# VectorE's block sums, key copies and additions in another order, and raw products placed ahead, in attention followed by two matrix products

## The chip, the cores and the metric

The kernel runs on one core of a Trainium2 chip. The metric is the device time of one execution in microseconds (us). The kernel before took a median of 229.66 us over 5 runs (229.41 to 230.65). A difference of 0.3%, that is 0.69 us, is about what a measurement of this kernel can tell from no change.

The core has five engines, each with its own queue that it works off strictly in order. TensorE (PE) multiplies matrices: it first loads a 128x128 block as weights (PEld), then streams the other operand past it, and its results land in PSUM, a small memory of 8 banks. VectorE (DVE) and ScalarE (ACT) work element by element and empty PSUM into SBUF, the main on-chip memory. GpSimd (POOL) and SyncE (SP) serve here mostly to start DMA transfers. Engines wait for each other through semaphores.

## The reference

```python
# attention, 4 batches x 8 heads x 768 positions x 64; q, k, v are given as float32
scores = (q @ k^T) / 8
mask   = causal for heads 0, 2, 6 ; causal and (first 4 keys or the last 64 keys) for heads 1, 3, 4, 5, 7
a      = exp(scores - max) / (sum + 1e-9), masked scores at -1e9
x      = (a @ v) with heads side by side: 3072 tokens x 512
# two products
h   = x @ w_in          # 512 x 2048
g   = max(0.01*h, h)
out = g @ w_out         # 2048 x 512, float32
```

The kernel computes in bf16 with float32 accumulation.

## The kernel before

**Chunks.** The 3072 tokens are cut into 8 chunks of 384 (half a batch each). `ORDER` (line 57) lists them; "chunk n" is the n-th in that order. Chunks 0 and 1 are the first halves of batches 0 and 1, chunks 2 and 3 their second halves, 4 and 5 the first halves of batches 2 and 3, 6 and 7 their second halves. A chunk goes through three parts.

**Attention of chunk n** (class `Attention`, line 294) is a list of "slots". One slot is a score product (L345 for the heads with full causal attention, L380 for the heads with a window, L325 for the first 4 "sink" keys) into one of two PSUM banks named `psS`, the exponential on ACT (L350, L385, L328), a multiplication with a mask on DVE (L355, L353, L389), and, `lag` slots later, the product with the values (L314) into the banks `po`. When the two heads of one quarter (p = 0 to 3) are done, DVE takes the reciprocal of the sums (L411) and scales (L413, tile `xs`). The result has to be transposed into `xt`: for chunks 1 and 2 by TensorE (L423, emptied by ACT at L425), from chunk 3 on by a DMA on the SP queue (L418).

**Keys and queries.** q, k and v are loaded by POOL's queue (L119, L124) and, from chunk 2 on, turned by DMA transposes on the SP queue (L244): queries into `qd`, keys into `kd`. From `kd` DVE copies the keys into the tiles `kt` that the score products read: six copies of 64x512 per chunk (L253, function `spreads`), and for the first half of a batch two small copies of the sink keys (L278, L282).

**Product 1 of chunk n** (`in_slots`, line 580) is 16 groups of 4 matmuls (L584) into the banks `ph`; ACT applies the leaky ReLU and writes `g_all` (L587). The four matmuls of a group read the four quarters of `xt`, one each.

**Product 2** works on pairs of token tiles of 128. Each chunk has three tiles: two of them make a pair of their own, the third waits for the third tile of the following chunk. So there are 12 pairs: pair 0 from chunk 0, pairs 1 and 2 after chunk 1, pair 3 from chunk 2, pairs 4 and 5 after chunk 3, and so on. Cut into 2x2 blocks, a pair would be eight block products; it is done as seven "units" P1 to P7 in Winograd's way, of 8 matmuls each (L648). They need four sums of the left factor, S1 to S4 (L631, function `sum`, on DVE), and four sums of the weights made once (L609). S2 needs S1, and S4 needs S2. A unit is cut into two steps of 4 matmuls. The units of a pair use three accumulators in PSUM:

- "a": P1, emptied by ACT into `p1` (L667), then P2 on top, emptied by ACT into the output tile `o` (L672);
- "y": P6, emptied by DVE with `p1` added into `u`; then P7 on top, emptied into `u3`; then P4 on top, emptied into `o` (all L663);
- "x": P5, emptied with `u3` added into `o`; then P3 on top, emptied with `u` added into `o`.

So P7 waits until DVE has read P6, P4 until it has read P7, and P3 until it has read P5. P1 and P2 need no sum: they read `g_all` itself ("raw products"). P6 needs S2, P7 S3, P5 S1, P3 S4. Pairs share the two banks `py`. The rows go out by SP's queue (L660).

**What sets the order.** The schedule is written out by hand: every call appends to its engines' queues, in the order of the program. `steps(k, units)` is the list of steps of pair k; `merge(ms, as_)` deals the slots `as_` of the next chunk's attention among the steps `ms` in proportion to costs written at the steps (0.44 for half a unit, 0.65 for a group of product 1); `last_of(ms, us)` gives how many steps are left out at the end, as `keep`, to be run after the attention. A sum of the following pair is emitted after P5, P4 and P3 of a pair (S1, S2, S3), S4 after P1 (line 711 on).

Three stretches matter below:

1. After product 1 of chunk 1: P6, P2, P7, P5, P4, P3 of pair 0 with the key copies of chunk 2 (lines 906 to 910), then S1 to S4 of pair 1 (911), then attention of chunk 2 dealt among 16 steps: pair 1's P6, P7, P5, P4, P3 and pair 2's P1, P6, P2 halves (915 to 918), then the key copies of chunk 3 (919).
2. Attention of chunk 3 beside product 1 of chunk 2, then P5, P4, P3 of pair 2, P1, P6, P2, P7 of pair 3 (`run(outs[:8])`, 940), with the key copies of chunk 4 (`extra`, line 954) emitted ahead of them.
3. Attention of chunk 4 dealt among the groups of product 1 of chunk 3, followed by P5, P4, P3 of pair 3. `last_of(ms, 5.8)` (950) takes P5, P4, P3 and 5 groups out of the dealing.

Of the kernel before, what the change touches and what calls it, by code (L numbers as in the profile page):

```python
# [21 lines left out]
def kernel(  # L22
# [21 lines left out]
    NG = DF // 128  # L44
# [27 lines left out]
    half = one.tile([128, 2], FP32, name="half")  # L72
# [498 lines left out]
    done = [0] * NCH  # L571
# [4 lines left out]
    def costing(us, f):  # L576
        f.us = us
        return f
# [117 lines left out]
    pairs = []  # L696
# [4 lines left out]
        if n % 2:  # L701
            pairs.append(Pair((n - 1, spare(n - 1)), (n, spare(n)), ("psS", "po", "py ph") if end else ("py", "py", "py"), end))

    def steps(k, units=Pair.UNITS, sums=True):

        r = []
        for u in units:
            for half in range(2):
                def step(u=u, half=half):
                    pairs[k].unit(u, half)  # L710
                    if half and u == "P1":
                        if sums:
                            pairs[k].sum(4)
                    if half and 0 < k < len(pairs) - 1 and u in ("P5", "P4", "P3"):
                        pairs[k + 1].sum({"P5": 1, "P4": 2, "P3": 3}[u])
                r.append(costing(0.44, step))
        return r

    def run(*lists):
        for l in lists:  # L720
            for f in l:
                f()
# [175 lines left out]
    for i in range(1, 5):  # L898
        pairs[0].sum(i)
    p1 = in_slots(1, ("ph", "psS"))  # L900
    run(p1[:14], steps(0, ("P1",), False), p1[14:])
    weight_sums(1)
    turn_dma(3)
    load_qk(4)
    load_v(4)
    run(steps(1, ("P1",), False), steps(0, ("P6", "P2", "P7")))
    sp = spreads(2)
    for i, u in enumerate(("P5", "P4", "P3")):
        run(steps(0, (u,)), sp[2 * i : 2 * i + 2])
    run(sp[6:])  # L910
    for i in range(1, 5):
        pairs[1].sum(i)
    run(steps(1, ("P2",)))
    v_shift(3)
    a2, m2 = Attention(2, xt_tag="ph").slots(lag=3), steps(1, ("P6", "P7", "P5", "P4", "P3")) + steps(2)
    m2, outs = m2[:16], m2[16:]
    at = last_of(m2, 2.6)
    run(merge(m2[:at], a2[:-6]), tail(m2[at:], a2[-6:]))
    run(spreads(3))
# [1 line left out]
    for n in range(2, NCH):  # L921
        a, extra = [], ()
        if n + 2 < NCH:
            turn_dma(n + 2)
            v_shift(n + 2)
            extra = spreads(n + 2)
            if ORDER[n + 2][1] == 0:
                load_sinks(ORDER[n + 2][0])
            if n + 3 < NCH:
                load_qk(n + 3, "k" if n > 2 else "kq")  # L930
                if n < 3:
                    load_v(n + 3)
            if ORDER[n + 2][1] == 0:
                sink_values(ORDER[n + 2][0], nc.gpsimd)
        if n + 1 < NCH:
            a = Attention(n + 1, cross=True).slots(lag=2 if n > 2 else 3)
            a = into(a, extra) if n > 2 else a
        ins = in_slots(n)
        if n == 3:
            run(outs[:8])  # L940
            ms = merge(ins, outs[8:8]) + outs[8:]
        else:
            lead = outs[:2] + ins[:2]
            ms = lead + merge(ins[2:], outs[2:-6]) + outs[-6:]
        keep = []
        if n == 2:
            at = last_of(ms, 3.5)
            ms, a, keep = ms[:at], a[:-3], tail(ms[at:-2], a[-3:]) + ms[-2:]
        elif a:
            at = last_of(ms, 5.8)  # L950
            ms, keep = ms[:at], ms[at:]
            if n > 4:
                keep.insert(1, a.pop())
        run(merge(ms, a), keep, extra if n == 2 else ())
        if n in (3, 4):

            nc.gpsimd.tensor_copy(hold[0:1, :], xts[n + 1][0:1, 3, 0:1])
            if n > 2:
                load_qk(n + 3, "q")
            load_v(n + 3)  # L960
        outs = [f for k in range(3 * n // 2, 3 * n // 2 + 1 + n % 2) for f in steps(k)]
# [36 lines left out]
```

## Time and profile before

| | |
|---|---|
| median of 5 runs | 229.66 us (229.41 to 230.65) |
| the profiled execution's own time | 229.72 us |
| its span, first to last instruction | 227.90 us (1.82 us lie around it) |
| granted TensorE clock | 1.00 |
| busy in the span: PE / PEld / DVE / ACT / POOL | 217.2 / 166.4 / 134.6 / 134.6 / 71.4 us |
| a half unit of product 2 (4 matmuls, start to next start) | 0.44 us |
| a group of product 1 (4 matmuls, start to next start) | 0.65 us |
| S1 to S4 on DVE, one | 0.68 us |
| key copy on DVE, median of 36 / longest | 0.29 / 0.93 us |

How to read the lines of the profile: a line of the timeline has start and duration in us, the engine, the line of the kernel, the operation, the tiles written and read, the shape, and how many instructions are merged; in brackets the idle time of the engine ahead of it and whose work ended that. Matmuls overlap, so the time of one is longer than the distance to the next. A DMA's line stands when its queue issues it; when it lands is told as a distance from the issue.

### The profile page before, as it was taken

The numbers are of one execution on the slowest core, as the hardware profiler recorded it, in microseconds if no ns is written. First come the engines' busy times: TensorE is split into PE (matmuls) and PEld (weight loads), VectorE is DVE, ScalarE is ACT, GpSimd is POOL, SyncE is SP. The second block draws the span as 40 slices with busy tenths as digits, with TensorE's granted clock in tenths as the row PEclk, the third lists the DMA queues.
The fourth block names the chain that finished last, engine by engine and source line by source line (L and its number), as shares of the span: only waits on it lengthen the run. The fifth ranks groups of instructions, "written<-read, shape, count | busy, mean of one in ns | idle before, by whom it ended". The sixth has DMA issues, their size and how long they took to land.

```text
span 227.9 us, 5799 instructions
## 1 busy us (share of the span) xinstructions
PE 217.2 (95%) x2344; PEld 166.4 (73%) x2344; DVE 134.6 (59%) x373; ACT 134.6 (59%) x300; POOL 71.4 (31%) x88
## 2 busy tenths in 40 slices
PE   8998899997999999699999999999999999999994
PEld 5687776685788677577688778777777877767893
DVE  7785958948589244948374774454353563600773
ACT  5676856742795996168647543888467774355110
POOL 8978534208508509506080402600000000000000
PEclk9999999999999999999999999999999999999999
DMA  9999999999999999999999991999220032200222
GB/s 130 156 176 168 199 207 174 179 148 135 151 104 271 181 175 152 135 216 160 92 123 153 159 206 25 184 116 151 55 92 3 19 86 60 92 3 0 92 95 92
DMA packets 112970, 29.14 MB, mean 128 GB/s; under 512 B 102960, under 2 KB 110000, under 8 KB 112944
## 3 DMA queue, kind: packets, MB, share of 16 engines
q0 software_dynamic: 77552, 13.37, 86.9%
q1 hardware_dynamic: 34336, 15.14, 35.1%
q8 instruction: 18, 0.29, 0.6%
q10 hardware_dynamic: 1056, 0.26, 0.5%
q14 instruction: 8, 0.07, 0.1%
HBM read 27.30 MB, written 6.29 MB: 147 GB/s over the span
## 4 chain that ended last, share of the span: by engine, by line
PE 80%; DVE 8%; DMA 6%; POOL 2%; issue 1%; ACT 1%; POOLq 0%
PE ph L584 32%; PE py L648 24%; PE po L314 7%; PE psS L345 5%; DMA w_in_bf<-in_moe_w_in_dram 4%; PE po L648 3%; DMA va<-in_v_dram 2%; PE psS L584 2%; DVE sum L631 2%; PE psS L380 2%; DVE kt L253 2%; PE psS L648 2%; PE psS L325 2%; POOL va L124 2%; DVE o L663 1%
## 5 line engine op out<-in xcount | busy, mean ns | idle before, releaser
L584 PE MATMUL ph<-xt,w_in_bf 128*128 128x384 bf16 x448 | 87.8, 326 | 0.4 <-DMA w_in_bf<-in_moe_w_in_dram 0.4
L587 ACT ACTIVATE g_all<-ph 128x384 bf16<-128x384 f32 x112 | 54.9, 490 | 32.6 <-PE ph L584 31.5
L584 PEld LDWEIGHTS <-w_in_bf 128*128 128x128 bf16 x480 | 42.9, 97 | 21.6 <-issue 0.6
L350 ACT ACTIVATE at<-psS 128x384 bf16<-128x384 f32 x78 | 36.8, 490 | 15.3 <-PE psS L345 14.0
L648 PEld LDWEIGHTS <-sum 128*128 128x128 bf16 x400 | 36.8, 98 | 10.6 <-issue 2.6
L119 POOL DMA_DIRECT2D kb<-in_k_dram x21 | 18.8, 914 | 47.3 <-DMA kd<-kb 46.6
L648 PEld LDWEIGHTS <-g_all 128*128 128x128 bf16 x288 | 27.2, 98 | 4.1
L648 PE MATMUL py<-w_out_bf,sum 128*128 128x256 bf16 (+1 forms) x176 | 24.0, 270 | 2.3 <-DVE u L663 2.3
L648 PE MATMUL py<-w_sum,sum 128*128 128x256 bf16 (+1 forms) x176 | 23.9, 270 | 1.2 <-DVE sum L631 1.2
L345 PE MATMUL psS<-qd,kt 128*128 128x384 bf16 (+2 forms) x90 | 22.7, 294 | 0.2
L124 POOL DMA_DIRECT2D va<-in_v_dram x24 | 21.3, 910 | 2.4 <-DMA w_out_bf<-in_moe_w_out_dram 1.8
L663 DVE TENSOR_TENSOR u<-py,p 128x256 f32<-128x256 f32 x20 | 8.4, 421 | 22.2 <-PE py L648 18.8
L119 POOL DMA_DIRECT2D qb<-in_q_dram x21 | 18.7, 910 | 6.1 <-DMA w_in_bf<-in_moe_w_in_dram 2.6
L648 PE MATMUL py<-w_out_bf,g_all 128*128 128x256 bf16 x144 | 20.2, 272 | 0.0
L314 PE MATMUL po<-va,at 128*128 128x65 bf16 x228 | 19.2, 194 | 0.0
L389 DVE TENSOR_TENSOR ats<-ats,m_win 128x384 bf16<-128x384 bf16 x35 | 12.2, 356 | 9.5 <-ACT ats L385 9.1
L385 ACT ACTIVATE ats<-psS 128x384 bf16<-128x384 f32 x35 | 16.6, 488 | 1.8 <-PE psS L380 1.5
L314 PEld LDWEIGHTS <-at 128*128 128x128 bf16 x234 | 14.8, 98 | 3.5
L631 DVE TENSOR_TENSOR sum<-g_all 128x1024 bf16<-128x1024 bf16 x24 | 16.4, 682 | 0.0
L663 DVE TENSOR_TENSOR o<-py,u 128x256 f32<-128x256 f32 (+1 forms) x24 | 9.8, 410 | 10.9 <-PE py L648 10.6
L413 DVE TENSOR_TENSOR xs<-po,linv 128x384 bf16<-128x384 f32 x27 | 15.0, 557 | 0.9
L253 DVE COPY kt<-kd 64x512 bf16<-64x512 bf16 x36 | 12.4, 345 | 2.9 <-DMA kd<-kb 2.5
(168 smaller groups left out, 294.8 us busy)
## 6 DMA issues: line engine op xcount, KB each, us to landing
out_dram<-o SPq DMA_DIRECT2D x23, 256.0 KB, 3.2
va<-in_v_dram POOLq DMA_DIRECT2D x24, 128.0 KB, 8.5
kb<-in_k_dram POOLq DMA_DIRECT2D x21, 128.0 KB, 5.9
qb<-in_q_dram POOLq DMA_DIRECT2D x21, 128.0 KB, 6.5
w_out_bf<-in_moe_w_out_dram POOLq DMA_DIRECT2D x4, 512.0 KB, 12.9
w_in_bf<-in_moe_w_in_dram POOLq DMA_DIRECT2D x3, 512.0 KB, 8.7
vb<-va SPq DMA_DIRECT2D x8, 170.6 KB, 4.2
w_in_bf<-in_moe_w_in_dram POOLq DMA_DIRECT2D x2, 256.0 KB, 7.8
```

The source lines that it names most:

```text
L119: nc.gpsimd.dma_start(out=t[:, g], in_=nat[nm][b, c, :, :, g])
L124: nc.gpsimd.dma_start(out=va[b][:, 3 * c + g, :, 0:D], in_=nat["v"][b, c, :, :, g])
L253: nc.vector.tensor_copy(kt[b % 2][hh][r, :, o : o + 128], raw["kx", n][r, g])
L314: nc.tensor.matmul(o, lhsT=lhsT, rhs=rhs, start=first, stop=False, skip_group_check=True)
L345: nc.tensor.matmul(s[:, off : off + w], lhsT=kt[i][hh][:, p, 128 * kj : 128 * kj + 128], rhs=q_of(n, p, lo, CH), start=(j == 0), stop=(j = ...
L350: nc.scalar.activation(out=a[:, 0:off], in_=s[:, 0:off], func=ACTF.Exp, scale=SM)
L385: nc.scalar.activation(out=av_, in_=s[:, 0:CH].rearrange("p (j e f) -> p j e f", j=3, e=2), func=ACTF.Exp, scale=SM)
L584: nc.tensor.matmul(ph[:, 0:CH], lhsT=w_in_bf[:, g, 128 * t : 128 * t + 128], rhs=xts[n][:, g, :] if n else xts[0][:, :, g, :], start=(g == ...
L587: nc.scalar.activation(out=g_all[:, slab(n) : slab(n) + 3, t, :], in_=ph[:, 0:CH].rearrange("p (j t) -> p j t", j=3), func=ACTF.Prelu, alp ...
L631: nc.vector.tensor_tensor(self.s[i], x, y, op=op)
L648: nc.tensor.matmul(s[:, 0 : c1 - c0], lhsT=lhs[:, j, :], rhs=rhs[:, j, c0:c1], start=first and j == 0, stop=(j == NH - 1), skip_group_chec ...
L663: add = lambda o, t: nc.vector.tensor_tensor(o, s, t[:, c0:c1], op=ALU.add)
```

## The change

The change moves instructions; it adds and removes none. On TensorE 4690 rows of weight loads and matmuls stand in both built programs, on DVE 371, and the rows of the other queues are the same in number; SP and POOL issue the same DMAs in the same order. It has five parts.

- **Sums by a waiting list.** Sums S1 to S3 of the next pair go to a list and are emitted when product 1 of their chunks is complete. S4 of pair k (k > 1) is emitted after P7 of the pair and no longer after P1.
- **Pair 1's S1 and S2** are emitted during pair 0's units, after P2 and P7. S3 and S4 stay where they were.
- **The order of steps beside attention of chunk 2**: pair 2's P1, pair 1's P6, pair 2's P2, pair 1's P7, P5, P4, P3, pair 2's P6. P1 and P2 of pair 2, the raw products, move from places 11 to 12 and 15 to 16 to places 1 to 2 and 5 to 6 of the 16 steps; with them go their two evictions on ACT.
- **Key copies of chunk 4**: four of the six are emitted after pair 3's P2 and so behind DVE's reading of its P6; the other two and the sink copies after P7.
- **P5 of pair 3** is run ahead of product 1 of chunk 3. `ms` is so two steps shorter at its end, and `last_of(ms, 5.8)` now leaves out P4, P3 and 7 groups: attention of chunk 4 is dealt among 9 groups where it was dealt among 11.

```diff
-    def steps(k, units=Pair.UNITS, sums=True):
+    pending = []
+
+    def flush():
+        while pending and all(done[n] == NG for n, _ in pending[0][0].rows):
+            p, i = pending.pop(0)
+            p.sum(i)
+
+    def steps(k, units=Pair.UNITS):
...
                     pairs[k].unit(u, half)
-                    if half and u == "P1":
-                        if sums:
-                            pairs[k].sum(4)
-                    if half and 0 < k < len(pairs) - 1 and u in ("P5", "P4", "P3"):
-                        pairs[k + 1].sum({"P5": 1, "P4": 2, "P3": 3}[u])
+                    if not half:
+                        return
+                    if u == "P7" and k > 1:
+                        pairs[k].sum(4)
+                    if 0 < k < len(pairs) - 1 and u in ("P5", "P4", "P3"):
+                        pending.append((pairs[k + 1], {"P5": 1, "P4": 2, "P3": 3}[u]))
+                    flush()
...
-    run(steps(1, ("P1",), False), steps(0, ("P6", "P2", "P7")))
+    run(steps(1, ("P1",)), steps(0, ("P6", "P2")))
+    pairs[1].sum(1)
+    run(steps(0, ("P7",)))
+    pairs[1].sum(2)
...
-    for i in range(1, 5):
+    for i in range(3, 5):
         pairs[1].sum(i)
...
-    a2, m2 = Attention(2, xt_tag="ph").slots(lag=3), steps(1, ("P6", "P7", "P5", "P4", "P3")) + steps(2)
-    m2, outs = m2[:16], m2[16:]
+    m2 = steps(2, ("P1",)) + steps(1, ("P6",)) + steps(2, ("P2",)) + steps(1, ("P7", "P5", "P4", "P3")) + steps(2, ("P6", "P7", "P5", "P4", "P3"))
+    a2, m2, outs = Attention(2, xt_tag="ph").slots(lag=3), m2[:16], m2[16:]
...
         if n == 3:
-            run(outs[:8])
-            ms = merge(ins, outs[8:8]) + outs[8:]
+            run(outs[:6], extra3[:4], outs[6:8], extra3[4:], outs[8:10])
+            ms = ins + outs[10:]
...
-        run(merge(ms, a), keep, extra if n == 2 else ())
+        run(merge(ms, a), keep)
+        extra3 = extra
```

## The prediction

> **What bounds the kernel now.** I read the page first: TensorE (PE) is busy for 217.2 of 227.9 us, DVE and ACT for 59% each. So only a wait of PE is worth anything. The two longest waits of PE are these:
>
> ```profile
> PE 217.2 (95%) x2344; PEld 166.4 (73%) x2344; DVE 134.6 (59%) x373; ACT 134.6 (59%) x300; POOL 71.4 (31%) x88
> ...
> PE py L648 <- DVE u L663: 2.3, 2, 2.2
> PE py L648 <- DVE sum L631: 1.2, 1, 1.2
> ```
>
> Both lie in the stretches that the change touches. Next the timelines of PE and DVE there. At 55 us PE waits 1.22 us for S1 and S2 of pair 1, which DVE makes behind six key copies; at 95 us it waits 2.16 us because P7 of pair 3 needs DVE's reading of P6 (`u`), which stands behind six key copies and S4:
>
> ```profile
> 54.83 0.69 DVE L631 TENSOR_TENSOR sum<-g_all 128x1024 bf16<-128x1024 bf16 x1
> 55.55 0.69 DVE L631 TENSOR_TENSOR sum<-sum,g_all 128x1024 bf16<-128x1024 bf16 x1
> 56.30 0.61 PE L648 MATMUL py<-w_sum,sum 128*128 128x256 bf16 x4 [1.22 <-DVE sum L631]
> ...
> 93.41 2.44 DVE L253 COPY kt<-kd 64x512 bf16<-64x512 bf16 x6
> 96.63 0.41 DVE L663 TENSOR_TENSOR u<-py,p 128x256 f32<-128x256 f32 x1
> 97.09 1.03 PE L648 MATMUL py<-w_out_bf,sum 128*128 128x256 bf16 x8 [2.16 <-DVE u L663]
> ```
>
> A wait removed is a gain only if nothing later holds PE. So last I looked for what PE meets behind each wait, with the landings of the SP queue's transposes:
>
> ```profile
> L244 SPq DMA_TRANSPOSE qd<-qb x1: 3237/3237/3237, 63.2 to 63.2; - x1
> ...
> DMA to landing us min/median/max: 8.3/8.3/8.3
> ...
> 71.25 0.33 PE L423 MATMUL ph<-ident,xs 128*128 128x128 bf16 x3
> 71.55 0.34 PE L345 MATMUL psS<-qd,kt 128*128 128x384 bf16 x1
> ...
> L418 SPq DMA_TRANSPOSE xt<-xs x4: 1200/1206/2001, 86.6 to 91.3; - x4
> ...
> DMA to landing us min/median/max: 5.5/6.3/7.0
> ...
> 97.97 0.49 PE L345 MATMUL psS<-qd,kt 128*128 128x384 bf16 x3
> 98.29 0.49 PE L584 MATMUL ph<-xt,w_in_bf 128*128 128x384 bf16 x2
> ...
> 108.31 0.36 DVE L389 TENSOR_TENSOR ats<-ats,m_win 128x384 bf16<-128x384 bf16 x1
> ...
> 108.73 0.23 PE L314 MATMUL po<-va,ats 128*128 128x65 bf16 x2
> ...
> 108.99 4.24 PE L584 MATMUL ph<-xt,w_in_bf 128*128 128x384 bf16 x24
> ```
>
> A DMA's line (the views of the tiles `qd` and `xt`) gives the issue, the one below it the time from issue to landing. The queries of chunk 3, issued at 63.25, land 8.3 later at 71.5, and the first score of chunk 3 starts at 71.55, so PE is already held by that DMA (its transposes of `xs` end near 71.42). The last quarter of chunk 3's `xt`, issued at 91.28, lands 7.0 us later (the view narrowed to it), at 98.3; the fourth matmul of the first group, which needs it, starts at 98.29 + 3 x 0.16 = 98.78, half a us later.
>
> **Stretch 1 (55 to 71.5): 0.** S1 and S2 of pair 1 go into DVE's idle times at 49.7 and 51.3 (0.60 and 1.25 us idle in the timeline, against 0.60 us to the next start for a sum), and the first steps beside attention of chunk 2 need no sum. I followed the three queues in the order of the built program with the durations of the rows (score 0.16, half unit 0.44, exponential 0.41 to the next, sum 0.60, 0.2 from PE to a reader, 0.05 back); the same walk over the old order gives the old starts within 0.15 us. PE's wait of 1.22 goes. Part comes back: scores 3 and 4 now wait for the exponentials (0.14 and 0.25); the eviction of P2 on ACT (0.38) holds the bank of a later score (0.18); P6 of pair 2 waits for S2 of its pair, now just ahead of it on DVE (0.25). At the transposes PE is 1.1 us ahead, at about 70.3. There stands the DMA. Its chain (queries of chunk 2 landed at 54.5, POOL's loads from 55.07, landed at 63.1, SP's transpose at 63.25) has no step that PE, DVE or ACT sets, and SP's and POOL's order is unchanged. So the first score of chunk 3 stays at 71.55 and the 1.1 us become a wait at a new place. If the DMA landed sooner, P7 of pair 2 would still wait for `u`, now behind S3 on DVE, until 71.17 instead of 71.72: the bounds are -0.55 and 0, and I take 0, by the row of the landing. S4 of pair 2, now at 73.8 to 74.5, fits ahead of the mask at 74.68.
>
> [...]
>
> **Stretch 2a (94.8 to 98.3): the wait goes, the DMA stays.** `u` is now ahead of the copies: P6 ends at 93.9, `u` runs 94.1 to 94.5, and P7 starts at 94.77, where PE stands, P5 at 95.64, the scores of chunk 4 at 96.51. The second of these needs the fifth copy: four copies (0.31 each) to 95.7, `u3` at 95.84, S4 to 96.8, the copy to 97.1. So PE waits 0.5 there and then for the `xt` quarter: the fourth matmul of the first group starts at 98.30 instead of 98.78, and P5 is already done. If all behind stayed as it is, that were -0.48 - 0.87 = -1.35.
>
> **Stretch 2b (98.3 to 113): it comes back.** Attention of chunk 4 was dealt among groups that covered its chain score, exponential, mask, values. In the built order 10 groups stood ahead of its last value product and 6 behind; now 8 and 8. Where the two are missing PE waits:
> - h2's first score follows the sink product with no group between. Its bank is freed by an exponential of h1, behind the eviction of group 1 on ACT: 0.33; then h1's mask: 0.23. That eats the 0.48.
> - h3's mask stands on DVE behind the reciprocal and scaling of quarter 0 (0.22 + 0.47). It came at 102.82 to 103.18 and the value product at 103.23, with a group at 102.37 as cover. Its score comes no sooner (the same work is ahead of it); the cover of 0.65 is gone: 0.7.
> - h7's mask stands behind four key copies (0.85 and 1.15 a pair) and a scaling. It ended at 108.67, the product started at 108.73 after 0.2 of waiting; with one group fewer ahead: 0.8.
>
> So the last value product of chunk 4 ends at about 109.0, as before. The old 6 groups took 108.99 to 113.06, 0.68 each; two more are +1.36. P5, 0.87, is no longer behind them. Sum: +1.36 - 0.87 = **+0.49**. The same walk over the old order gives P5's start as 113.02 against 113.06, so I trust it to some 0.3 us. Its bounds: no wait added, -1.35; key copies at 0.93, the longest row, +0.8.
>
> The copies: two that ran beside POOL's work took 0.43 to 0.58 each there, against a median of 0.29; without that (0.54 less ahead of the mask of h7), the sum would be -0.05. POOL's work there follows the landing of a DMA and not PE, so I leave them slow.
>
> **The rest: 0.** S4 behind P7 in pairs 4 to 11: P7's reading starts 0.2 after P7, takes 0.34, S4 0.60, P5's reading 0.42, done at 1.57 after P7; P3 starts at 1.74 in the tightest case (P5, P4, P3 without a pause, as at 216). So no wait, 0.17 us to spare. In its old place S4 held no mask that PE waited for. Bounds -0.1 and +0.3.
>
> **Sum.** The profiled execution took 229.72 (span 227.90 and 1.82). +0.49 makes 230.21; it stood 0.06 above the median, so **230.15**, +0.2%. That is inside the 0.3% (0.69 us) that a measurement can tell.
>
> **Rivals.**
> - *Faster: the attention of chunk 4 packs closer than I reckon.* For it: the wait of 2.16 is gone and P5 is filled in. Against it: the walk meets the old times. It decides where the last value product of chunk 4 ends before 107.8; with the -1.35 in full the time is 228.3, with a sum of half the two -0.43, with the landing of stretch 1 besides -0.98: 228.7.
> - *Slower: chunk 3's `xt` lands later.* Its last quarter becomes the gate at 98.3, where there was 0.5 to spare. It is issued by the same steps, but into full DMA queues, and the four of that chunk differ by 1.5 us. Each 0.1 later is 0.1 more: half that spread makes +0.74, 230.9. It decides from a landing at 98.5.
> - *The gain of stretch 1 comes through* because the queries land sooner: 230.15 - 0.55 = 229.6. Against it: nothing in that chain is touched.
>
> **How the numbers follow.** The forecast 0.47 (its own range 229.5 to 230.7), faster rival 0.20, slower rival 0.25, stretch 1 through 0.08. Within 0.3% (228.97 to 230.35): most of the forecast, 0.40, and the last rival, 0.08: 0.48. Slower: 0.25 and 0.07 of the forecast, 0.32. Faster: 0.20. Range 228.7 to 231.0, the faster rival's middle to a little over the slower one's price.
>
> **What would show it.** Right: no PE wait at 55 and at 95; a wait of 1 us or more ahead of chunk 3's first score, which stays near 71.5; P7 of pair 3 right behind P2; a wait at the fourth matmul of product 1 of chunk 3 or the score before it; waits of some 0.7 ahead of value products of chunk 4, eight groups of product 1 in a row behind them, and P4 of pair 3 near 114.4, later than its old 113.94. Wrong: chunk 3's first score before 71, or P4 of pair 3 before 113.3.

## The result, and the profile after

The changed kernel takes 229.71 us (median of 39 executions), the kernel before 230.76 us (65 executions, taken beside them). The ratio is 0.9958, with a 95% interval of 0.9942 to 0.9975: faster by 0.42%, about 0.97 us (0.58 to 1.34). The forecast was 0.49 us slower. The five executions that the forecast started from (median 229.66) lay about a microsecond under the median of the 65, and that turns out to be part of the cause. The ratios leave out executions that took over 1.5% longer than the fastest of the same kernel; in the four sets below these are ten of the kernel before, all at a lower granted clock (0.985 to 0.993), so the ratios rather understate what such a clock costs.

The profile after does not show the gain at first sight. Its span is longer than that of before (227.9). The page, span and busy times:

```profile
span 228.2 us, 5798 instructions
...
PE 217.6 (95%) x2344; PEld 165.5 (73%) x2344; DVE 134.1 (59%) x373; ACT 134.8 (59%) x300; POOL 71.2 (31%) x88
```

The waits of TensorE in the profile after (us in total, times, longest):

```profile
PE po L219 <- DMA kb<-in_k_dram: 1.5, 3, 0.7
...
PE po L314 <- DVE ats L389: 0.8, 2, 0.5
...
PE py L648 <- DVE u L663: 0.6, 1, 0.6
```

The first line lies at 18 to 20 us, in code that the change doesn't touch: the keys of chunk 1 landed later in this execution. So one profile of each kernel can't be compared by the span. I cut each execution at three places on TensorE: the first score of chunk 2, P7 of pair 2, P4 of pair 3. The differences between them are taken from the timelines.

| profile | first score of chunk 2 at | to P7 of pair 2 | to P4 of pair 3 | to the end | mean clock |
|---|---|---|---|---|---|
| before | 54.59 | 17.13 | 42.22 | 113.96 | 1.000 |
| after | 55.63 | 16.56 | 41.90 | 114.11 | 1.000 |

After is 1.04 us late before the change begins, gains 0.57 in stretch 1, gains 0.32 in stretch 2 and loses 0.15 behind. The timeline of TensorE in the profile after, in the two stretches:

```profile
55.63 0.50 PE L345 MATMUL psS<-qd,kt 128*128 128x384 bf16 x2
55.96 0.60 PE L648 MATMUL py<-w_out_bf,g_all 128*128 128x256 bf16 x4
...
71.12 0.33 PE L423 MATMUL ph<-ident,xs 128*128 128x128 bf16 x3
71.28 0.33 PE L345 MATMUL psS<-qd,kt 128*128 128x384 bf16 x1
72.19 0.60 PE L648 MATMUL py<-w_out_bf,sum 128*128 128x256 bf16 x4 [0.58 <-DVE u L663]
...
94.35 1.04 PE L648 MATMUL py<-w_out_bf,g_all 128*128 128x256 bf16 x8
95.23 1.04 PE L648 MATMUL py<-w_out_bf,sum 128*128 128x256 bf16 x8
96.10 1.04 PE L648 MATMUL py<-w_sum,sum 128*128 128x256 bf16 x8
96.97 0.44 PE L345 MATMUL psS<-qd,kt 128*128 128x384 bf16 x2
...
97.64 0.98 PE L584 MATMUL ph<-xt,w_in_bf 128*128 128x384 bf16 x4
...
103.24 0.24 PE L314 MATMUL po<-va,ats 128*128 128x65 bf16 x2 [0.52 <-DVE ats L389]
...
108.37 0.24 PE L314 MATMUL po<-va,ats 128*128 128x65 bf16 x2 [0.30 <-DVE ats L389]
...
108.63 5.63 PE L584 MATMUL ph<-xt,w_in_bf 128*128 128x384 bf16 x32
114.09 1.04 PE L648 MATMUL py<-w_sum,g_all 128*128 128x256 bf16 x8
```

Both waits of before are gone: raw products follow the first scores at 55.96, and P7 of pair 3 stands right behind P2 at 95.23. Chunk 3's first score at 71.28 follows the transposes without a wait; it is P7 of pair 2 that waits, for `u`. Behind the last value product, which starts at 108.57, there are eight groups in a row, 32 matmuls, as forecast. The two DMA transposes that the forecast watched (views of the tiles `qd` and `xt`; issue in us, and below it the time to landing):

```profile
L244 SPq DMA_TRANSPOSE qd<-qb x1: 1633/1633/1633, 63.8 to 63.8; - x1
...
DMA to landing us min/median/max: 5.9/5.9/5.9
```

```profile
L418 SPq DMA_TRANSPOSE xt<-xs x4: 1204/1206/2493, 86.3 to 91.5; - x4
...
DMA to landing us min/median/max: 5.9/6.8/6.8
```

The queries landed 5.9 us after their issue and not 8.3, so they held nothing here. The last quarter of `xt` landed at 98.26, where the fourth matmul of the group that began at 97.64 stands, as forecast.

### The profile page after: what moved, and what is told of

Same layout as the page of the kernel before. It is cut to its first block, busy times and chain, and to the rows that moved or that the text cites. A ratio compares the mean times of both kernels' runs of the same rounds, so it can differ in the third digit from the quotient of the medians.

```text
span 228.2 us, 5798 instructions
## 1 busy us (share of the span) xinstructions
PE 217.6 (95%) x2344; PEld 165.5 (73%) x2344; DVE 134.1 (59%) x373; ACT 134.8 (59%) x300; POOL 71.2 (31%) x88
## 4 chain that ended last, share of the span: by engine, by line
PE 67%; DMA 13%; POOL 7%; DVE 5%; issue 4%; ACT 2%; SPq 0%; POOLq 0%; ACTq 0%
PE ph L584 27%; PE py L648 20%; PE po L314 6%; PE psS L345 4%; DMA kb<-in_k_dram 4%; DMA kd<-kb 4%; DMA w_in_bf<-in_moe_w_in_dram 4%; PE po L648 3%; POOL va L124 2%; PE psS L584 2%; PE psS L380 2%; DVE o L663 2%; PE psS L648 2%; DMA qb<-in_q_dram 1%; PE psS L325 1%
## 5 line engine op out<-in xcount | busy, mean ns | idle before, releaser
L631 DVE TENSOR_TENSOR sum<-g_all 128x1024 bf16<-128x1024 bf16 x24 | 17.1, 712 | 0.0
L314 PEld LDWEIGHTS <-ats 128*128 128x128 bf16 x210 | 10.2, 97 | 5.0 <-DVE ats L389 2.4
L253 DVE COPY kt<-kd 64x512 bf16<-64x512 bf16 x36 | 11.8, 327 | 2.5 <-DMA kd<-kb 2.0
```

Of the source, the lines that this page charges most:

```text
L314: nc.tensor.matmul(o, lhsT=lhsT, rhs=rhs, start=first, stop=False, skip_group_check=True)
L631: nc.vector.tensor_tensor(self.s[i], x, y, op=op)
```

## The experiments

All runs in one table: medians with the number of executions, the ratio to the kernel before on the same chip, and in how many executions the mean granted clock was below 0.9965. In the four sets of the kernel before that was so in 51 of 118 executions. A set is what was taken on one chip side by side: the first four rows, the next four, and so on. Ratios of different sets are compared below only by their intervals.

| run | median us | before us | ratio (95%) | low clock |
|---|---|---|---|---|
| before_again | 230.05 (12) | 230.72 (35) | 1.0001 (0.9967 to 1.0036) | 5 of 12 |
| after_again | 229.18 (12) | 230.72 (35) | 0.9941 (0.9914 to 0.9969) | 1 of 12 |
| st1_alone | 230.42 (12) | 230.72 (35) | 0.9993 (0.9965 to 1.0022) | 8 of 12 |
| st2_alone | 230.65 (12) | 230.72 (35) | 1.0023 (0.9993 to 1.0053) | 2 of 12 |
| before_warm | 229.95 (12) | 230.94 (35) | 0.9973 (0.9941 to 1.0004) | 2 of 12 |
| s4_alone | 229.73 (12) | 230.94 (35) | 0.9960 (0.9930 to 0.9991) | 0 of 12 |
| wait_back | 232.82 (12) | 230.94 (35) | 1.0071 (1.0035 to 1.0107) | 4 of 12 |
| no_p5 | 228.92 (12) | 230.94 (35) | 0.9929 (0.9893 to 0.9964) | 2 of 12 |
| s4_st1 | 229.02 (7) | 231.07 (13) | 0.9919 (0.9877 to 0.9962) | 0 of 7 |
| deal11 | 228.28 (6) | 231.07 (13) | 0.9878 (0.9835 to 0.9920) | 0 of 6 |
| best_deal | 227.19 (6) | 231.07 (13) | 0.9832 (0.9790 to 0.9874) | 0 of 6 |
| best_nop5 | 228.86 (7) | 231.07 (13) | 0.9910 (0.9875 to 0.9944) | 1 of 7 |
| warm_both | 229.88 (12) | 230.31 (35) | 0.9983 (0.9953 to 1.0012) | 0 of 12 |
| st1_warm | 229.46 (12) | 230.31 (35) | 0.9962 (0.9936 to 0.9987) | 0 of 12 |
| st2_warm | 230.23 (12) | 230.31 (35) | 0.9998 (0.9968 to 1.0028) | 0 of 12 |
| after_third | 230.27 (12) | 230.31 (35) | 0.9987 (0.9953 to 1.0020) | 1 of 12 |

### Both kernels a second time, and each half of the change alone

The two kernels were run again without an edit, for second profiles.

> The kernel before, unchanged, for a second profile of it. Four milestones of TensorE divide the execution: the first score of chunk 2 (54.59 us before, 55.63 us after), P7 of pair 2 (17.13 us later before, 16.56 after), P4 of pair 3 (42.22 us later before, 41.90 after), the end of the span (113.96 us later before, 114.11 after). Theory 1 (the head of the execution varies by chance): the first score of chunk 2 comes between 54.5 and 56 us and not where the first profile has it, and the two middle stretches stay at 17.1 and 42.2 within 0.3 us. Theory 2 (the two stretches themselves vary as much as the two profiles differ): 17.13 or 42.22 moves by 0.4 us or more.

> The changed kernel, unchanged, for a second profile. Theory 1 (the stretches are what the change moved): 16.6 us from the first score of chunk 2 to P7 of pair 2, 41.9 from there to P4 of pair 3, and 0.9 to 1.0 us less than before in the median. Theory 2 (the landing of the queries of chunk 3 decides, as the prediction had it): 17.1 in this profile, and 0 to 0.4 us less than before in the median.

The part for stretch 1 alone keeps S4 of pair 3 on in its old place and takes these edits:

```diff
                     if half and u == "P1":
-                        if sums:
+                        if sums and k > 2:
                             pairs[k].sum(4)
+                    if half and u == "P7" and k == 2:
+                        pairs[k].sum(4)
...
-    run(steps(1, ("P1",), False), steps(0, ("P6", "P2", "P7")))
+    run(steps(1, ("P1",), False), steps(0, ("P6", "P2")))
+    pairs[1].sum(1)
+    run(steps(0, ("P7",)))
+    pairs[1].sum(2)
...
+    m2 = steps(2, ("P1",)) + steps(1, ("P6",)) + steps(2, ("P2",)) + steps(1, ("P7", "P5", "P4", "P3")) + steps(2, ("P6", "P7", "P5", "P4", "P3"))
```

> The kernel before with the part of the change for stretch 1 alone: S1 and S2 of pair 1 early, the new order of the 16 steps, S4 of pair 2 behind its P7. By the prediction (the DMA of the queries of chunk 3 holds TensorE) it takes as long as before, 0.0 us, and chunk 3's first score follows that landing; by its bound -0.55 us, with P7 of pair 2 held by the reading of P6. By the two profiles -0.57 us: 16.6 us from the first score of chunk 2 to P7 of pair 2. If what is won is lost again at the next wait (P7 of pair 3, 2.16 us), 0.0 us in the median although the stretch is shorter.

The part for stretch 2 alone takes these:

```diff
+                    if u == ("P7" if k > 2 else "P1") and k > 1:
+                        pairs[k].sum(4)
...
-            run(outs[:8])
-            ms = merge(ins, outs[8:8]) + outs[8:]
+            run(outs[:6], extra3[:4], outs[6:8], extra3[4:], outs[8:10])
+            ms = ins + outs[10:]
```

> The kernel before with the part for stretch 2 alone: four key copies of chunk 4 behind the reading of P6 of pair 3, P5 of pair 3 ahead of product 1 of chunk 3, S4 of pairs 3 to 11 behind P7. By the prediction +0.49 us, P4 of pair 3 42.7 us after P7 of pair 2. By the two profiles -0.3 us, 41.9 us. By the prediction's bound, with no wait of the attention of chunk 4 added, -1.35 us.

Measured, each half alone was no faster than the kernel before (-0.07% and +0.23%, each with an interval of 0.3 either way; +0.23% is 0.5 us, near what the forecast said of stretch 2), while both together gained 0.59% in the same set, some 1.4 us (0.7 to 2.0) and above what either theory had. The milestones of these profiles:

| profile | first score of chunk 2 at | to P7 of pair 2 | to P4 of pair 3 | to the end | mean clock |
|---|---|---|---|---|---|
| before_again | 53.82 | 17.64 | 43.75 | 113.99 | 0.993 |
| after_again | 53.81 | 16.87 | 42.28 | 114.14 | 1.000 |
| st1_alone | 54.16 | 16.75 | 44.30 | 113.99 | 0.993 |
| st2_alone | 53.85 | 18.09 | 42.26 | 114.20 | 1.000 |

The same kernel took 42.22 us in stretch 2 once and 43.75 the other time, so theory 2 of the first run held. The first profile of before was the lucky one: its clock was 1.00 throughout. What makes the difference is in the timeline of TensorE in the second profile of before, behind the wait at 95 us:

```profile
96.95 1.17 PE L648 MATMUL py<-w_out_bf,sum 128*128 128x256 bf16 x8 [2.26 <-DVE u L663]
97.92 0.85 PE L345 MATMUL psS<-qd,kt 128*128 128x384 bf16 x3
98.56 1.49 PE L584 MATMUL ph<-xt,w_in_bf 128*128 128x384 bf16 x4
```

A group of product 1 takes 1.49 us here and 0.81 in the first profile, three scores 0.85 and 0.49. The windows of one microsecond give the reason (PEclk, the entry behind POOL's, is the granted clock):

```profile
core 0: us, PE busy (x) PEld busy (x) DVE busy (x) ACT busy (x) POOL busy (x), PEclk, DMA share, GB/s
...
96.00:97.00 1.00, 0.05 (x1) 0.04 (x1) 0.90 (x2) 0.00 (x0) 0.00 (x0) 1.00 1.90 209
97.00:98.00 1.00, 1.00 (x9) 0.86 (x9) 0.00 (x0) 0.00 (x0) 0.00 (x0) 0.86 1.45 281
98.00:99.00 1.00, 1.00 (x6) 0.60 (x5) 0.42 (x1) 0.52 (x2) 0.00 (x0) 0.50 1.39 245
99.00:100.00 1.00, 1.00 (x7) 0.50 (x6) 0.52 (x2) 0.35 (x1) 0.00 (x0) 0.50 1.60 156
100.00:101.00 1.00, 1.00 (x14) 0.82 (x12) 0.01 (x1) 0.87 (x2) 0.00 (x0) 0.50 1.60 160
101.00:102.00 1.00, 1.00 (x10) 0.70 (x9) 0.34 (x1) 0.38 (x1) 0.00 (x0) 0.94 1.59 158
```

The granted clock falls to 0.50 shortly after the wait has ended. Read with one step from 1.00 to 0.50 and one back, 0.86 puts the fall at 97.72 and 0.94 the return at 101.12: 3.4 us at half speed. The profile of stretch 1 alone shows the same from 97.34 to 100.74. In the kernel before, the executions with such a mean clock took 231.11 us against 229.79 for the others (15 and 17 executions of this set), 1.3 us more.

So a new theory, A: the wait of 2.2 us costs its length in every execution, and in about four of ten also 1.3 us behind it. Its rival, B: the low clock is chance and the wait costs its length alone. The set above already speaks for A: stretch 1 alone keeps the wait at 95 us and had the low clock in 8 of 12 executions, stretch 2 alone is without it and had it in 2.

### Is it the wait that lowers the clock?

First, the kernel before with the wait left where it is, but filled with matmuls of zeros:

```diff
-            run(outs[:8])
+            run(outs[:6])
+            idle("psS", 14)
+            run(outs[6:8])
```

> The kernel before with 14 matmuls of zeros (128x256, 0.107 us each, 1.5 us in all, into a free bank that nothing reads) put into TensorE's wait of 2.2 us ahead of P7 of pair 3; the wait for the reading of P6 stays, and with it the start of P7. Theory A (the granted clock falls to half for 3.4 us behind this wait in some executions, which costs 1.3 us each time): no execution with a mean clock of 0.991 to 0.993, where the kernel before had them in about half, and a median 0.6 us lower, 229.7 to 230.1 us. Theory B (a wait costs its length and no more, the low clock is chance): the same share of executions at 0.993 and the same time, 0.0 us.

2 of 12 executions had the low clock, against 18 of 35 of the kernel before in this set, and the ratio was 0.9973 (its interval just touches 1). Theory A had asked for none. They may come from the other wait, at 55 us, so that one was filled too:

```diff
+    first = m2[0]
+    m2[0] = costing(first.us, lambda: (idle("ph", 10), first()))
```

> The kernel before with matmuls of zeros in both waits of TensorE: 10 (1.1 us) in the wait for S1 and S2 of pair 1 at 55 us, 14 (1.5 us) in the wait for the reading of P6 of pair 3 at 95 us. Nothing reads what they write. If the low clock comes from these two waits alone, no execution has a mean clock below 0.996, where 2 of 12 had it with the second wait alone filled, and the time lies at the full-clock executions of the kernel before, about 0.6 us below its median. If it has another source, one or two of 12 executions stay low.

None of 12, and none in the 24 executions of the two variants below, in which also both waits are filled or gone; the kernel before had the low clock in 11 of 35 in this set. (2 and 0 of 12 alone would not tell the two runs apart.) The mean of the 12 is 229.95 us; the 24 executions of the kernel before at full clock in this set had 229.90, and all 35 had 230.54. The timeline of TensorE with both filled shows the zeros in the place of the idle time (14 in 1.69 us, 0.11 from one start to the next) and P7 where it was:

```profile
94.96 1.69 PE L157 MATMUL psS<-blank 128*128 128x256 bf16 x14
97.39 1.03 PE L648 MATMUL py<-w_out_bf,sum 128*128 128x256 bf16 x8 [0.73 <-DVE u L663]
```

Nothing useful was added, the wait for `u` still ends at the same place, and the low clock is gone. That settles it against B: in this kernel the idle time lowers the clock. It need not be these two waits alone: without them the changed kernel still had the low clock in 2 of 64 executions.

Second, the wait made shorter. S4 of pair 3 stood ahead of `u` on DVE; moved behind P7, in pairs 3 to 11 and with nothing else:

```diff
-                        if sums:
+                        if sums and k == 2:
                             pairs[k].sum(4)
+                    if half and u == "P7" and k > 2:
+                        pairs[k].sum(4)
```

> The kernel before with S4 of pairs 3 to 11 behind P7 and nothing else. At P7 of pair 3 this takes S4 (0.60 us) out of the wait of 2.2 us, which leaves 1.6. By the prediction: the 0.5 us to spare at the last quarter of xt are lost again, -0.1 to 0.0 us, and no effect elsewhere. By theory A (a wait of 2.2 us lets the clock fall in half of the executions, one of 1.6 us does so less often): fewer executions at 0.993 than in the kernel before and 0.3 to 1.0 us less in the median.

```profile
97.25 1.03 PE L648 MATMUL py<-w_out_bf,sum 128*128 128x256 bf16 x8 [1.66 <-DVE u L663]
```

In that timeline the wait is 1.66 us and P7 runs at full speed (8 matmuls in 1.03 us, as in the first profile of before). None of 12 executions had the low clock, and the ratio is 0.9960, within its interval the same as that of the whole change. By the prediction's working this edit was worth 0.1 us at most.

Third, the wait put back into the changed kernel, with P5 of pair 3 and everything else as changed:

```diff
-                    if u == "P7" and k > 1:
+                    if u == ("P1" if k == 3 else "P7") and k > 1:
                         pairs[k].sum(4)
...
-            run(outs[:6], extra3[:4], outs[6:8], extra3[4:], outs[8:10])
+            run(extra3, outs[:10])
```

> The changed kernel with all key copies of chunk 4 and S4 of pair 3 put back ahead of the reading of P6 of pair 3, so that the wait of 2.2 us ahead of P7 is there again; everything else as changed, P5 ahead too. Theory A: the mean clock of 0.991 to 0.993 comes back in about half of the executions, and those take 1.3 us more than the others; the median lies 0.6 us or more above the changed kernel's. Theory B: the wait only moves the same work, 0 to 0.5 us more than the changed kernel, no execution at 0.993.

The low clock came back in 4 of 12 executions. In the timeline of TensorE P5 takes 1.91 us where it took 1.04:

```profile
98.72 1.58 PE L648 MATMUL py<-w_out_bf,sum 128*128 128x256 bf16 x8 [2.33 <-DVE u L663]
100.10 1.91 PE L648 MATMUL py<-w_sum,sum 128*128 128x256 bf16 x8
```

Both theories missed the size: the ratio rose from 0.994 for the changed kernel (another set) to 1.0071, some 3 us, and even the executions at full clock took 231.9 us. In the new order P5 too stands behind the wait, and P5 and the scores fall into the low clock. That nothing behind takes the wait up, so that it counts in full, would explain the 231.9; it was not tried by itself.

### What each half is worth at full clock

With the waits filled the clock no longer blurs the parts. The part for stretch 1 with the wait at 95 us filled, and the part for stretch 2 with the wait at 55 us filled, each beside the kernel before with both filled; and the changed kernel in the same set.

> The part of the change for stretch 1 alone, with the 14 matmuls of zeros in the wait at 95 us. Against the run with both waits filled this is the worth of stretch 1 at full clock. By the prediction 0.0 us (bound -0.55); by the profiles (17.6 us with the old order, 16.9 with the new, from the first score of chunk 2 to P7 of pair 2) -0.6 us.

> The part of the change for stretch 2 alone, with the 10 matmuls of zeros in the wait at 55 us. Against the run with both waits filled this is the worth of stretch 2 at full clock. By the prediction +0.49 us; by the profiles at full clock (42.2 to 42.4 us from P7 of pair 2 to P4 of pair 3 in the order before, 41.9 to 42.3 as changed, and 0.15 us more behind P4) +0.1 us, within 0.3.

> The changed kernel, beside the three runs that take it apart. If the parts add up at full clock: the run with both waits filled, plus what the parts for stretch 1 and stretch 2 each differ from it. By the two sums: -0.5 us against the run with both waits filled (theory of this text, -0.6 and +0.1), +0.5 us by the prediction.

The means of 12 executions are 229.95 us with both waits filled, 229.52 with stretch 1 changed (-0.42, 95% interval 0.42 either way) and 230.33 with stretch 2 changed (+0.38, 0.47 either way). The changed kernel's 11 executions at full clock had 229.81 (-0.13, 0.61 either way). So at full clock the halves nearly cancel in this set. Within these intervals the forecast's +0.49 for stretch 2 stands, and stretch 1 lies nearer to its bound of -0.55 than to the 0 that I took.

The executions at full clock of the first set look different: against those of the kernel before, stretch 1 alone lies 0.29 us lower (0.39 either way), stretch 2 alone 0.96 higher (0.64) and the whole change 0.77 lower (0.47). There the parts don't add up to the whole. So the runs show that the clock is a part of the gain; how large a part they leave open.

The same part for stretch 1, on top of the kernel in which S4 alone was moved:

```diff
-                        if sums:
-                            pairs[k].sum(4)
+                    if half and u == "P7" and k > 1:
+                        pairs[k].sum(4)
...
+    m2 = steps(2, ("P1",)) + steps(1, ("P6",)) + steps(2, ("P2",)) + steps(1, ("P7", "P5", "P4", "P3")) + steps(2, ("P6", "P7", "P5", "P4", "P3"))
```

> S4 of pairs 2 to 11 behind P7, and the part for stretch 1; key copies and P5 as in the kernel before. With the run that moved S4 alone (no execution below a clock of 0.998) this shows what stretch 1 is worth where the clock stays up. By the prediction (the landing of chunk 3's queries holds TensorE) 0.0 us against that run: 0.40% faster than before. By the profiles (17.6 us from the first score of chunk 2 to P7 of pair 2 in five profiles with the old order, 17.0 in five with the new) 0.3 to 0.6 us less than that run: 0.55 to 0.65% faster than before.

Its ratio is 0.9919 against 0.9960, from 7 executions and in another set; the intervals overlap, but the direction is that of the run before. Over the profiles, stretch 1 took 17.13, 17.64, 17.69, 17.45, 18.09, 17.65 and 18.13 us in the old order (mean 17.7) and 16.56, 16.87, 16.75, 16.46, 17.56, 17.32, 16.85, 17.30 and 17.03 in the new (mean 17.0; the two runs at the end, which move more sums, are not counted).

### What dealing the attention among fewer groups costs

P5 of pair 3 put back behind product 1 of chunk 3, so that 11 groups are dealt again:

```diff
-            run(outs[:6], extra3[:4], outs[6:8], extra3[4:], outs[8:10])
-            ms = ins + outs[10:]
+            run(outs[:6], extra3[:4], outs[6:8], extra3[4:])
+            ms = ins + outs[8:]
```

> The changed kernel with P5 of pair 3 back behind product 1 of chunk 3, so that attention of chunk 4 is dealt among 11 groups again. By the prediction dealing among 9 groups adds waits of 0.7 and 0.8 us ahead of value products and P5 ahead fills 0.87 us beside the xt transpose; without both, P7 and the scores come sooner and PE waits for the last quarter of xt near 98.3: 0.5 us less than the changed kernel. By the profile after, where those waits measured 0.52 and 0.30 us: 0.0 us, within 0.3. No execution at a clock of 0.993 either way.

And P5 left ahead, but 11 groups dealt:

```diff
-            at = last_of(ms, 5.8)
+            at = last_of(ms, 4.5 if n == 3 else 5.8)
```

> The changed kernel with attention of chunk 4 dealt among 11 groups of product 1 of chunk 3 (5 groups left behind it and not 7), P5 of pair 3 still ahead. By the prediction's working (waits of 0.7 and 0.8 us ahead of value products because two groups of cover are gone) it is 1.0 to 1.4 us faster than the changed kernel, P4 of pair 3 41 us after P7 of pair 2. By the profile after, where PE waits 0.17, 0.52 and 0.30 us at these places, at most 1.0 us faster. If the masks come no sooner and only the place of the wait moves, 0.0 us.

Without P5 ahead the ratio is 0.9929 (changed kernel 0.9958; the intervals overlap), with 11 groups dealt 0.9878, whose interval lies below that of the changed kernel. The forecast for the first also missed the clock: 2 of its 12 executions had the low one. Its profile has a wait of 1.27 us for a key copy at 97.09; whether that wait is longer in those two is not known. The timeline of TensorE with 11 groups dealt:

```profile
98.65 0.32 PE L584 MATMUL ph<-xt,w_in_bf 128*128 128x384 bf16 x1 [0.58 <-DMA xt<-xs]
...
108.61 4.24 PE L584 MATMUL ph<-xt,w_in_bf 128*128 128x384 bf16 x24
112.69 1.04 PE L648 MATMUL py<-w_sum,g_all 128*128 128x256 bf16 x8
```

The last value product starts 36.6 us after P7 of pair 2, as in the profile after (36.4), but two more groups stand ahead of it and 24 matmuls behind it in place of 32. Stretch 2 takes 40.73 us and not 41.90 to 42.28. The waits for masks were filled with groups, as the forecast's working of stretch 2 had it, and the place of the price is shown. In the times it is 0.8% or 1.8 us, across two sets and more than was expected; what lies beyond the 1.2 us of the stretch is not accounted for.

### A version faster than both

The last two add what was learnt: 11 groups dealt (or P5 not ahead), S4 of pair 3 behind all its key copies, and the sums of pair 2 made before they are needed, since in the profile after P7 of pair 2 waits 0.58 us for `u` behind S3.

```diff
-                    if u == "P7" and k > 1:
+                    if u == "P7" and k > 1 and k != 3:
                         pairs[k].sum(4)
-                    if 0 < k < len(pairs) - 1 and u in ("P5", "P4", "P3"):
+                    if (k, u) in ((1, "P6"), (2, "P2"), (1, "P5")):
+                        pairs[2].sum({"P6": 1, "P2": 2, "P5": 3}[u])
+                    if 1 < k < len(pairs) - 1 and u in ("P5", "P4", "P3"):
...
-            run(outs[:6], extra3[:4], outs[6:8], extra3[4:], outs[8:10])
+            run(outs[:6], extra3[:4], outs[6:8], extra3[4:])
+            pairs[3].sum(4)
+            run(outs[8:10])
...
-            at = last_of(ms, 5.8)
+            at = last_of(ms, 4.5 if n == 3 else 5.8)
```

> The changed kernel with attention of chunk 4 dealt among 11 groups; S4 of pair 3 behind all key copies; and S1, S2, S3 of pair 2 made earlier (behind P6 of pair 1, P2 of pair 2, P5 of pair 1), so that P6 of pair 2 doesn't wait 0.22 us for S2 and P7 not 0.58 us for the reading of P6 behind S3. Expected over the run with 11 groups alone: 0.5 us less, if the landing of chunk 3's queries allows it (it held the first score in one of the five profiles with the new order); 0.0 if the queries hold.

> The changed kernel without P5 ahead, with S4 of pair 3 behind all key copies (the third score of chunk 4 waited 1.27 us for a key copy behind S4 in the run without P5 ahead), and with the earlier sums of pair 2. TensorE then waits at the last quarter of xt of chunk 3 (97.68 us in that run's profile, where the fourth matmul started at about 97.7), so S4's place brings 0.0 us by that landing and up to 0.6 us where it lands sooner; the sums 0.5 us. If the wait ahead of xt grows over 2 us, executions at a clock of 0.993 come back.

With 11 groups dealt and P5 ahead it takes 227.19 us against 231.07, a ratio of 0.9832 (0.9790 to 0.9874): faster than both kernels. Against the run with 11 groups alone, in the same set, its mean of 6 executions is 1.1 us lower (0.95 either way), where 0.5 was expected; which of the two additions does it was not tried. The second variant, without P5 ahead and with `last_of` as changed, has 0.9910, in another set than the run without its two additions (0.9929), and not clear of it. In the timeline of the faster one the two DMAs of the forecast are the longest waits left from 50 to 116 us:

```profile
71.81 0.34 PE L345 MATMUL psS<-qd,kt 128*128 128x384 bf16 x1 [0.48 <-DMA qd<-qb]
...
98.61 0.32 PE L584 MATMUL ph<-xt,w_in_bf 128*128 128x384 bf16 x1 [0.86 <-DMA xt<-xs]
...
112.64 1.04 PE L648 MATMUL py<-w_sum,g_all 128*128 128x256 bf16 x8
```

## Why the prediction was wrong

| term of the sum | forecast | measured |
|---|---|---|
| stretch 1 | 0 (bounds -0.55 and 0) | -0.42, 0.42 either way |
| stretch 2, with what lies behind it | +0.49 (bounds -1.35 and +0.8) | +0.38, 0.47 either way |
| the clock behind the wait at 95 us | not in the sum | -0.5 |
| sum | +0.49 | about -0.55; the change itself -0.97 (-0.58 to -1.34) |

The third line is worked out: 51 of 118 executions of the kernel before had the low clock and 2 of 64 of the changed one, 0.43 less 0.03, times the 1.1 to 1.6 us that such executions took more in the four sets. The parts do not quite reach the whole; their intervals are as wide as the rest, and I leave that open, as also the 0.77 us that the first set gave the change at full clock.

- **The step that failed** is the price of the wait in stretch 2a: each wait of PE counts for its length, -0.48 and -0.87 there, and the sum has no term for the clock. The wait of 2.16 us had a second price, 1.1 to 1.6 us in 43% of the executions, some 0.5 us on average, that the one profile of before did not show, since its clock was 1.00. With the 0.42 that stretch 1 brought where the sum had 0, it turns the sign. S4 moved alone, which takes 0.6 us out of that wait, brings about as much as the whole change. The forecast had read the time from five executions and not asked why one of them took 230.65 and another 229.41. That its 230.15 us lies only 0.44 from the 229.71 measured is luck: it started a microsecond below the median of the kernel before and added where the change took off.
- **Stretch 1: 0 was the wrong end.** The step "there stands the DMA" rested on one landing, 8.3 us after the issue. The queries of chunk 3 landed 8.3 us after their issue in before, 7.2 in its second profile, 5.9 in after and 7.8 in best_deal, and they held the first score by more than 0.2 us in two of eleven profiles with the new order (0.48 in best_deal, 0.30 in after_third). In eight of the others what holds is the step named as the bound: P7 of pair 2 waits for `u` behind S3 on DVE, 0.58 us, as in the profile after (the last one, best_nop5, makes S3 earlier). It came 16.56 us after the first score of chunk 2, 0.57 sooner than before.
- **Stretch 2a: the order was right**, the clock aside. P7 of pair 3 stands behind P2, P5 at 96.10, and the fourth matmul of the first group at the landing of the last quarter of `xt` (98.26). The wait for the fifth copy was 0.17 and not 0.5.
- **Stretch 2b: right in kind, too long by half a microsecond.** The waits ahead of value products measured 0.52 and 0.30 where 0.7 and 0.8 were reckoned. The second is short because the two copies ahead of that mask took 0.78 and not 1.15; POOL's work moved with the landing that releases it (106.51 in place of 106.87). That was the point at which I chose to leave the copies slow. Eight groups stood behind, as reckoned, and dealing 11 groups takes 1.2 us out of the stretch.
- **The rest: 0 was missed by 0.15 to 0.2, inside its bounds and for a reason not named.** In the eight profiles with P5 ahead, 114.11 to 114.21 us lie behind P4 of pair 3; in nine without, 113.94 to 114.04 (best_nop5 has 114.86, which was not followed up). With P5 ahead of product 1, S1 of pair 4 has to wait until product 1 of chunk 3 is complete, and the three sums run into the mask of chunk 5's first value product. DVE in the profile after:

```profile
115.51 0.68 DVE L631 TENSOR_TENSOR sum<-g_all 128x1024 bf16<-128x1024 bf16 x1
...
117.17 0.68 DVE L631 TENSOR_TENSOR sum<-g_all 128x1024 bf16<-128x1024 bf16 x1
117.77 0.22 DVE L355 TENSOR_TENSOR at<-at,m_caus 128x128 bf16<-128x128 bf16 x1
```

The mask stands 3.68 us behind P4 of pair 3; before it stood 3.01 behind it (116.95 and 113.94), and TensorE's value product comes 0.18 later.

- **The rivals.** "Faster" came out, but not by its mechanism: the last value product of chunk 4 started at 108.57, far from 107.8. "The gain of stretch 1 comes through" is what happened in stretch 1. "Slower, by a later `xt`" did not happen: its last quarter landed at 98.26 in both first profiles.
- **The signs.** Neither sign of being wrong came in the profile after: chunk 3's first score stood at 71.28 (not before 71) and P4 of pair 3 at 114.09 (not before 113.3). But this execution was 1.04 us late before the change begins; counted from the first score of chunk 2, both signs came. A sign told as a distance would have shown it.

## What to carry to other kernels

An idle stretch of TensorE cost more than its length here: one of 2.2 us (2.16 and 2.26 in the two profiles of before) went with a low clock in 51 of 118 executions, 3.4 us of it in the profile that holds it, and shortening it by half a microsecond, alone, brought about as much as the whole change. Look at the spread of the times and at the granted clock of each execution before a single profile is taken for the kernel; a bimodal time asks for its cause. And when a step is moved out of a merged list, ask what it covered there: giving the dealing its 11 groups back took 1.2 us out of the stretch, where the whole change is worth 0.97.

## What the runs showed of the hardware

**The clock.** The low clock lasted 3.4 us in each of the three profiles that hold it: from 97.72 us in the second profile of before, 97.34 in stretch 1 alone, 99.06 with the wait put back, by the windows of one microsecond. Over a span of 228 us one such fall makes a mean clock of 0.993, two make 0.985; both stand among the executions. The waits ahead of the three falls were 2.26, 2.27 and 2.33 us; in the 3.4 us ahead of the fall TensorE had still been busy for 1.15, 1.1 and 1.1. The wait that was 1.66 us in the profile with S4 moved alone went with no low clock in 12 executions. A longer one did not always lower it: in the profile of stretch 2 alone TensorE waits 2.31 us for S1 and S2 up to 56.66, and the windows from 53 to 61 us all have a granted clock of 1.00.

The places of the falls tell something of why the same wait lowers the clock in one execution and not in the next. In the second profile of before the clock falls once more at the end, when TensorE has run out of work. By windows of 0.2 us, finer than those above, the first fall is at 97.71 and the last at 230.83:

```profile
97.60:97.80 0.20, 0.20 (x4) 0.18 (x2) 0.00 (x0) 0.00 (x0) 0.00 (x0) 0.78 1.80 255
...
230.70:230.90 0.20, 0.00 (x0) 0.00 (x0) 0.00 (x0) 0.00 (x0) 0.00 (x0) 0.83 0.00 0
```

That is 133.12 us apart. In the first profiles the trace's entries of the clock begin at 6.97 us (before) and 4.10 (after), and the fall at the end is at 228.83 and 229.38: 221.87 and 225.28 us, which differ by 3.41. The three distances are 39, 65 and 66 times 3.413 us. An estimate from these three: the clock changes at steps of 3.41 us, which start at another place in each of the three profiles (0.69, 0.14 and 2.14 us into the span for after, before and its second profile).

With that step, counted back from 228.83, the borders in the first profile of before lie at 95.71 and 99.13 and cut the wait of 2.16 us into 0.78 and 1.38, and the clock stayed up. In the second profile, counted back from 97.71, the wait of 2.26 us lies whole in one piece and the clock fell at its end; a piece around the wait at 55 us has 1.86 us idle, and the windows there show 1.00. In the other two profiles with a fall the waits of 2.27 and 2.33 us lie whole in the 3.41 us ahead of it. Apart from the end, where TensorE has no work left, no piece of the first profiles of before and after has more than 1.38 us idle. So of these pieces those with 2.26 us or more idle end in a fall and those with 1.86 or less don't; what lies between, and where the borders cut the 2.31 us of stretch 2 alone, is not shown.

An estimate from these numbers, the step of 3.41 and the 1.86 that did nothing: a wait of 2.16 us lies whole within one piece in (3.41 - 2.16) / 3.41, 37% of its places, and has more than 1.86 us in one piece in 54%; 43% of the executions showed the low clock. Apart from the 1.66 us above, no run varied the length of the wait to test it.

**DVE beside POOL.** Of the six key copies of chunk 2 five take 0.27 to 0.29 us; the first, beside POOL's issues of loads, took 0.38 in before (at 52.21, POOL's from 51.62 on) and 0.43 in after (53.61, POOL's from 52.17 on). Beside POOL's multiplication for the sink values near 93 us the six key copies there took 2.44 us in before, one of them 0.93, and 2.55 in the second profile of before and in that of stretch 1 alone. In the profile after it was a sum of the next pair, 1.41 us where a sum takes 0.68, while DVE's readings of PSUM ahead of it and behind it (92.93 and 94.62) kept their 0.42:

```profile
93.09 1.03 POOL L134 TENSOR_TENSOR vs<-vsf,m_sink 32x448 bf16<-32x448 f32 x1
93.27 1.41 DVE L631 TENSOR_TENSOR sum<-g_all 128x1024 bf16<-128x1024 bf16 x1
```

This is read off the timelines; no run tried it.

**The head of the execution.** The first score of chunk 2 came between 53.81 and 55.63 us in the 18 profiles. In the latest of them, the profile after, TensorE waited 1.5 us for the keys of chunk 1; what sets the others was not followed up. This spread of 1.82 us alone is 0.8% of the time, more than the change moved.
